# A load planner that charges for late loads by a graded curve, and the load order found with it

## The chip, the cores and the metric

The kernel runs on one core of a Trainium2 chip. The metric is the device time of one execution in microseconds (us). Before: 639.15 us, median of 4 runs (638.66 to 639.34). The experiments ran on three chips in as many sets of rounds, each with its own runs of before (medians 639.28, 638.76 and 639.18), so a kernel is compared by its ratio to before of the same rounds. A difference of two such ratios from different rounds is uncertain by about 0.25%, or 1.5 us.

## The reference

Two layers of attention with a KV cache and of a gated feed-forward block, each run twice with the same weights and the same caches, for four sequences and one new token.

```python
B, Sq, D = 4, 1, 512;  Hq, Hkv, Sk, Dh = 32, 8, 8192, 128;  F = 1792
x = A_x
x = x + attention(layernorm(x), k_cache, v_cache, wq, wo)   # layer 0
x = x + (silu(h @ w_gate) * (h @ w_up)) @ w_down             # h = layernorm(x)
x = x + attention(layernorm(x), k_cache, v_cache, wq, wo)   # layer 1, the same caches
x = x + feed_forward(layernorm(x))
```

Each cache is 64 MiB (4 x 8 x 8192 x 128 in bf16) and is read in both layers. SBUF holds only a small part of one.

## The kernel before

The caches are cut into units of 1 MB (1.049 MB in the profile's decimal count): half the rows of one head of one sequence, 8 KB in each of 128 partitions. SBUF has 11 slots for units (and 4 more in wq's place, once the last query is made). One DMA queue, issued from SyncE (SP), brings units into slots. A K unit is transposed in its slot by VectorE (2.3 us) and multiplied with the query by TensorE, a V unit is multiplied with the softmax by TensorE, and then the slot is free for a later load.

The code is shortened; `...` and the comments are this text's.

```python
def load_pair(u):                     # one unit; load_two does the same for two neighbours
    kind, l, b, g, cp = u             # K or V, layer, sequence, head, half
    def fn():
        s = PL.slot[home[u]]
        T.dma("sp", slot_sb(s), rows_of(u)[:, cp, :], sem_slot[s], writes=...)
    home[u] = u
    return PL.load(2.505, fn, u)
# ...
def t(hs): ...                        # k_pair: e.transpose(v, v) on DVE (L606)
def qk(): ...                         # 64 small matmuls into the score banks (L622)
st = PL.add("pe", 1.95, qk, tr + [qd, prev] + ..., prio, n=64)
if u not in kept_k:
    st.slot_of = home[u]              # after this step the slot is free
```

The order of loads is a string. `P` is two K units in one load, `K` one, `aBGH` a V unit of layer 0, `bBGH` one of layer 1, `A..` and `B..` two V units in one load, and `cBGH` a V unit of layer 1 that is *kept*: layer 0 left it in its slot, so nothing is loaded. `KM` says how many K units of each sequence are kept so. A kept unit saves 1 MB of reading and holds a slot meanwhile.

```python
ORDER = ("c100 c101 P c260 x P c300 c301 c261 wq P wg1 ... b360 b320 B35 B31 B33 b361 ")
KM = (4, 0, 0, 0)
```

Before the program is written, a planner runs through all steps with a duration for each, chooses slots and PSUM banks, and fixes the sequence of instructions on each engine. Each engine then works strictly in that sequence. The planner's times are used for these choices alone, and by whoever searched for the string. Its DMA model is this:

```python
LOAD_LEAD = 2.1
LOAD_TAIL = 2.1
# in pump(): t is when the load is issued, s.us how long its bytes take
dma_at = max(dma_at, t + self.LOAD_LEAD) + s.us    # end of transfer
s.end = dma_at + self.LOAD_TAIL                    # landing: what waits for it may start
```

## Time and profile before

| | before | how it is read |
|---|---|---|
| span of the profiled run | 636.9 us | first to last instruction of the core |
| cache and weight queue | 256.14 MB | the table of DMA queues |
| rate between the holes | 417 GB/s | table of stretches, 196 to 624 us |
| hole at the hand-over to layer 1 | 3.5 us | bytes missing against 417 GB/s, 184 to 196 us |
| last landing to end | 10.65 us | landing records: 626.25, span 636.9 |
| VectorE, TensorE busy | 63%, 62% | engine shares; neither is the bound |

One word is used throughout. The **lead** of a load is the time from its issue to the landing of the load before it in the queue. With a long lead, the bytes of this load follow those of its forerunner without a gap. Landings are read from the packed trace: a load has landed when its semaphore has had all of the load's 16 updates.

### The profile page before, as it was taken

To read this page: it belongs to the slowest core of one execution; us is meant where nothing else is said; L and a number is where in the kernel's file an instruction comes from. 1 tells how busy PE (TensorE), PEld (TensorE's weight loads), DVE (VectorE), ACT (ScalarE), POOL (GpSimd) and SP (SyncE) were. 2 spreads that over 40 slices of the span, in tenths; PEclk is the share of its full clock that TensorE was granted. 3 is DMA by queue.
4 is the path that set the end of the run, shared out by engine and by line. 5 is a ranking of instruction groups with operands and counts; after the bars stand their busy time and mean duration, and the time that the engine had idled before them with its cause. 6 is when DMAs were issued, how large, how long until landed. Compare 5 with 4: busy or idle time off the path is not lost.

```text
span 636.9 us, 18609 instructions
## 1 busy us (share of the span) xinstructions
PE 397.1 (62%) x8689; PEld 205.1 (32%) x8689; DVE 402.7 (63%) x615; ACT 40.4 (6%) x107; POOL 1.8 (0%) x8
## 2 busy tenths in 40 slices
PE   0375444454786675677576665578667676856686
PEld 0221211113542141135421241333431244721265
DVE  4477764365236958876579777366667863489832
ACT  1000200002000020000200100000100020000100
POOL 1000000000000000000000000000000000000000
PEclk9997686657557767667667778555575667568686
DMA  8999999999989999999999999999999999999991
GB/s 356 423 426 412 405 417 423 420 418 401 387 348 400 422 418 419 420 412 421 402 408 419 422 425 428 417 408 420 418 408 421 415 419 421 417 409 419 423 425 65
DMA packets 37237, 257.32 MB, mean 404 GB/s; under 512 B 3492, under 2 KB 9384, under 8 KB 10664
## 3 DMA queue, kind: packets, MB, share of 16 engines
q1 hardware_dynamic: 37160, 256.14, 97.7%
q8 instruction: 68, 1.11, 0.7%
q14 instruction: 9, 0.07, 0.0%
HBM read 256.12 MB, written 0.00 MB: 402 GB/s over the span
## 4 chain that ended last, share of the span: by engine, by line
DMA 63%; PE 18%; DVE 16%; issue 2%; SPq 0%; ACT 0%
DMA pool<-in_A_k_cache_dram 39%; DMA pool<-in_A_v_cache_dram 18%; DVE pool L606 12%; PE ps L622 7%; PE ps L763 5%; DMA wq_sb<-in_A_wq_dram 3%; PE ps L472 2%; DMA wo_sb<-in_A_wo_dram 2%; DMA wq_sb<-in_A_k_cache_dram 2%; DVE wq_sb L606 1%; PE ps L809 1%; PE ps L726 1%; DVE ps L790 1%; PE ps L681 1%; PE ps L873 1%
## 5 line engine op out<-in xcount | busy, mean ns | idle before, releaser
L606 DVE STREAM_TRANSPOSE pool<-pool 128x2048 uint32<-128x2048 uint32 x116 | 264.8, 2300 | 70.8 <-DMA pool<-in_A_k_cache_dram 70.6
L622 PE MATMUL ps<-pool,qpad 32*32 32x512 bf16 x3840 | 190.6, 543 | 127.2 <-DVE pool L606 120.7
L622 PEld LDWEIGHTS ps<-pool,qpad 32*32 32x32 bf16 x3840 | 54.6, 108 | 240.1 <-DVE pool L606 179.6
L763 PE MATMUL ps<-pool,pp 128*32 128x256 bf16 x1936 | 100.0, 366 | 43.1 <-DMA pool<-in_A_v_cache_dram 31.6
L763 PEld LDWEIGHTS ps<-pool,pp 128*32 128x32 bf16 x1936 | 57.5, 122 | 81.6 <-DMA pool<-in_A_v_cache_dram 42.8
L790 DVE STREAM_TRANSPOSE ps<-ps 128x256 f32<-128x256 f32 x62 | 28.4, 458 | 74.7 <-PE ps L763 74.4
L645 ACT ACTIVATE pp<-ps,negm 128x512 bf16<-128x512 f32 x32 | 21.6, 686 | 329.6 <-DVE negm L641 306.5
L726 PE MATMUL ps<-oT,wo_sb 128*128 128x4 bf16 x640 | 23.0, 167 | 12.6 <-DVE oT L794 9.2
L726 PEld LDWEIGHTS ps<-oT,wo_sb 128*128 128x128 bf16 x640 | 20.7, 103 | 24.7 <-DVE oT L794 16.7
L641 DVE TENSOR_REDUCE negm<-ps 128x1 f32<-128x512 f32 x32 | 19.9, 683 | 12.1 <-PE ps L622 12.1
L472 PE MATMUL ps<-xnT,wq_sb 128*128 128x4 bf16 x640 | 18.3, 166 | 12.1 <-DMA wq_sb<-in_A_wq_dram 11.4
L472 PEld LDWEIGHTS ps<-xnT,wq_sb 128*128 128x128 bf16 x640 | 17.7, 104 | 14.5 <-DMA wq_sb<-in_A_wq_dram 11.5
L606 DVE STREAM_TRANSPOSE wq_sb<-wq_sb 128x2048 uint32<-128x2048 uint32 x8 | 18.1, 2290 | 3.5 <-DMA wq_sb<-in_A_k_cache_dram 3.4
L681 PE MATMUL ps<-ident,pp 128*128 128x128 bf16 x128 | 16.0, 311 | 6.3 <-DVE pp L670 5.8
L622 PE MATMUL ps<-wq_sb,qpad 32*32 32x512 bf16 x256 | 13.2, 547 | 8.5 <-DVE wq_sb L606 8.5
L458 ACT ACTIVATE lnv<-var,eps_sb 128x4 f32<-128x4 f32 x10 | 3.0, 298 | 218.0 <-DVE var L453 218.0
L681 PEld LDWEIGHTS ps<-ident,pp 128*128 128x128 bf16 x128 | 12.7, 143 | 12.5 <-DVE pp L670 7.6
L792 DVE TENSOR_REDUCE osum<-ps 128x4 f32<-128x32 f32 x62 | 11.9, 191 | 2.1
L794 DVE TENSOR_TENSOR oT<-osum,invL 128x4 bf16<-128x4 f32 x62 | 10.5, 169 | 2.1
L670 DVE TENSOR_SCALAR pp<-pp,alpha 128x512 bf16<-128x512 bf16 x32 | 9.0, 346 | 1.8 <-ACT alpha L663 1.8
L690 ACT ACTIVATE pp<-ps 128x1024 bf16<-128x1024 bf16 x8 | 8.2, 1024 | 26.9 <-PE ps L681 26.9
L438 PE MATMUL ps<-xx,onesm 128*128 128x32 f32 x20 | 6.3, 410 | 5.3 <-DVE xx L433 4.3
(68 smaller groups left out, 149.4 us busy)
## 6 DMA issues: line engine op xcount, KB each, us to landing
pool<-in_A_k_cache_dram SPq DMA_DIRECT2D x86, 1024.0 KB, 9.7
pool<-in_A_v_cache_dram SPq DMA_DIRECT2D x82, 1024.0 KB, 10.0
pool<-in_A_k_cache_dram SPq DMA_DIRECT2D x15, 2048.0 KB, 15.8
pool<-in_A_v_cache_dram SPq DMA_DIRECT2D x10, 2048.0 KB, 16.6
wq_sb<-in_A_k_cache_dram SPq DMA_DIRECT2D x6, 1024.0 KB, 13.6
wq_sb<-in_A_wq_dram SPq DMA_DIRECT2D x1, 4096.0 KB, 22.0
wo_sb<-in_A_wo_dram SPq DMA_DIRECT2D x4, 1024.0 KB, 16.2
wq_sb<-in_A_k_cache_dram SPq DMA_DIRECT2D x1, 2048.0 KB, 10.3
```

The costliest lines, as they stand in the source:

```text
L472: op("pe", lambda e: e.matmul(ps[:, bk * BW + h * B:bk * BW + (h + 1) * B], lhsT=wq_sb[:, kt, h * Dh:(h + 1) * Dh], rhs=xnT[:, kt * B:(kt ...
L606: op("dve", lambda e: e.transpose(v, v), reads=keys, writes=keys)
L622: op("pe", lambda e: e.matmul(ps[32 * c:32 * (c + 1), a * BW:(a + 1) * BW], lhsT=qpad[rows, qbuf, es_, g, :], rhs=ap[h][rows, :, es_ // 2, ...
L641: op("dve", lambda e: e.tensor_reduce(negm[:, q, a:a + 1], bank(a), AX.X, ALU.max, negate=True), reads=[f"pb{a}"], writes=[f"negm{q}_{a}"])
L645: op("act", lambda e: e.activation(pblk(q)[:, :, a, :], bank(a).rearrange("p (t j) -> p t j", j=32), ACTF.Exp, bias=negm[:, q, a:a + 1], s ...
L670: op("dve", lambda e: e.tensor_scalar(seg, seg, alpha[:, q, a:a + 1], None, op0=ALU.mult), reads=[f"pp{q}_{a}", f"alpha{q}"], writes=[f"pp ...
L681: op("pe", lambda e: e.matmul(stg[:, t * P:(t + 1) * P], lhsT=pp[:, q, blk * P:(blk + 1) * P], rhs=ident[:], is_transpose=True, start=True ...
L726: op("pe", lambda e: e.matmul(ps[:, OPJ * BW + nq * B:OPJ * BW + (nq + 1) * B], lhsT=wo_sb[:, h, nq * P:(nq + 1) * P], rhs=oT[:, l, h, :], ...
L763: op("pe", lambda e: e.matmul(ps[32 * n:32 * (n + 1), bk * BW:bk * BW + 256], lhsT=pp[:, q, col:col + 32], rhs=v[:, 8 * f:8 * (f + 1), 32 ...
L790: op("dve", lambda e: e.transpose(blk, blk), reads=[f"pb{bk}"], writes=[f"pb{bk}"])
L792: op("dve", lambda e: e.tensor_reduce(osum[:], diag, AX.X, ALU.add), reads=[f"pb{bk}"], writes=["osum"])
L794: op("dve", lambda e: e.tensor_tensor(oT[:, l, g * REP:(g + 1) * REP, b], got, invL[:, q, g * REP:(g + 1) * REP], ALU.mult), reads=[f"pb{b ...
```

## The change

The intent, as far as the code shows it, is to charge a load by a graded curve of what a short lead costs, rather than by a hard limit, and to take an order and kept units found anew with it.

```diff
-    LOAD_LEAD = 2.1
+    LOAD_LEAD = 2.0
+    LOAD_SOFT = 1.05
+    LOAD_EASE = 3.7
     LOAD_TAIL = 2.1
...
+    def late(self, ahead):
+        if ahead < self.LOAD_LEAD:
+            return max(self.LOAD_LEAD - ahead, self.LOAD_SOFT)
+        return max(0.0, self.LOAD_SOFT * (self.LOAD_EASE - ahead) / (self.LOAD_EASE - self.LOAD_LEAD))
...
-                dma_at = max(dma_at, t + self.LOAD_LEAD) + s.us
+                dma_at += self.late(dma_at - t) + s.us
...
-ORDER = ("c100 c101 P c260 x P c300 c301 c261 wq P wg1 ...
+ORDER = ("P c200 x c201 c300 wq P c011 c260 P P a040 P c340 ...
-KM = (4, 0, 0, 0)
+KM = (2, 0, 0, 0)
...
-            return PL.load(4.914, fn, u0, u1)
+            return PL.load(4.924, fn, u0, u1)
-                return PL.load(2.505, fn, u)
+                return PL.load(2.51, fn, u)
```

## The prediction

> **What bounds the kernel now.** I read the page's engine shares and slice rows first. They say which resource is busy all the time.
>
> ```profile
> PE 397.1 (62%) x8689; PEld 205.1 (32%) x8689; DVE 402.7 (63%) x615; ACT 40.4 (6%) x107; POOL 1.8 (0%) x8
> ...
> DMA  8999999999989999999999999999999999999991
> GB/s 356 423 426 412 405 417 423 420 418 401 387 348 400 422 418 419 420 412 421 402 408 419 422 425 428 417 408 420 418 408 421 415 419 421 417 409 419 423 425 65
> ```
>
> No compute engine passes 63%. The DMA row is at 9 in all slices but the first, the twelfth and the last. So the kernel is one long read of the caches and weights, and its time is start + bytes over rate + holes in the stream + tail. The queue table gives the bytes, and the table of stretches (columns: length, then busy time of each engine with its instruction count, granted clock, DMA share, GB/s) gives rates and the one visible hole.
>
> ```profile
> q1 hardware_dynamic: 37160, 256.14, 97.7%
> ...
> 4.00:184.00 180.00, 91.12 (x2124) 48.17 (x2125) 99.77 (x145) 9.97 (x27) 0.00 (x0) 0.73 1.02 414
> 184.00:188.00 4.00, 3.02 (x60) 1.17 (x56) 2.54 (x2) 0.00 (x0) 0.00 (x0) 0.50 0.54 217
> 188.00:192.00 4.00, 4.00 (x116) 1.89 (x105) 0.82 (x3) 0.00 (x0) 0.00 (x0) 0.64 0.98 307
> 192.00:196.00 4.00, 2.48 (x104) 1.53 (x79) 0.00 (x0) 0.00 (x0) 0.00 (x0) 1.00 0.95 365
> 196.00:624.00 428.00, 286.97 (x6024) 143.43 (x6025) 295.32 (x441) 28.19 (x75) 0.00 (x0) 0.66 1.01 417
> 624.00:636.90 12.90, 9.47 (x314) 8.90 (x310) 3.99 (x22) 0.95 (x4) 0.00 (x0) 0.51 0.05 18
> ```
>
> Outside 184 to 196 us the stream runs at 414 to 417 GB/s, with the DMA share at 1. Inside it, (417 - 217) x 4 + (417 - 307) x 4 + (417 - 365) x 4 = 1448 KB are not moved, which is 1448 / 417 = **3.5 us**. The 12.9 us at the end are the last P·V products, the projection, the norm, the feed-forward part and the output. They need the last load and can't shrink by reordering.
>
> What opens the hole is in the chain that ended last (start, length, what) and in the timeline of the issuing queue:
>
> ```profile
> 165.11 0.18 DVE xx L889
> ...
> 174.56 2.07 PE ps L763 x25
> ...
> 180.93 1.88 PE ps L472 x64
> ...
> 184.05 0.98 PE ps L622 x16
> 185.03 0.98 issue
> 186.01 1.05 PE ps L622 x15
> ```
>
> ```profile
> 187.12 0.33 SPq L92 DMA_DIRECT2D pool<-in_A_v_cache_dram  x1
> ```
>
> The add of the attention result at 165.11 (L889) starts norm, feed-forward, norm and query projection (L472), with one V group of batch 1 in between (L763). The first score product of layer 1 (L622) ends at 187.06. It reads a kept K unit, and frees that unit's slot for the load issued at 187.12.
>
> **What the Trainium skill says.** "DMA: Bandwidth & Descriptors", section "Anatomy of one DMA — SWDGE (gpsimd) path", splits a DMA into a fixed part of about 2 us and a part that grows with the bytes. These loads are issued from SyncE, not GpSimd, but the hole looks like the same split: in the landing records the load before it was complete at 187.91 us, this load was issued at 187.12, only 0.79 us ahead, and it was complete at 193.66, 5.75 us after its forerunner instead of the usual 2.49. The loss of 3.25 us is larger than 2.0 - 0.79 = 1.2 us. The same page, "Rules for kernel authors", advises to issue a DMA early so that the setup overlaps. The trace agrees: the other cache loads were issued at least 3.9 us before their forerunner was complete, and none of them shows a loss of this kind. "TensorE: Matmul & The Clock Gate", section "What's actually happening", says that a little used TensorE runs at half clock. The table of stretches agrees (0.50 in 184 to 188), and the hand-over below is worked out at that clock.
>
> **The change, part by part.** It alters no instruction's form. It changes the planner's model of a late load, and with the new model another load order (a string of tokens), other kept units, and a little longer load constants were found. I take no time from either planner model, only counts and order of the emitted program.
>
> *Bytes.* A kept unit is a 1 MB half head of K or V that layer 0 leaves in SBUF for layer 1. Counting the tokens: before keeps 21 V and 4 K units, after keeps 22 V and 2 K units. So after loads one unit more: 232 instead of 231, and 257.19 MB instead of 256.14. At 417 GB/s this is 1.049 MB / 417 = **+2.5 us**, and it lies on the path, as DMA is the bound.
>
> *Pairs.* Double loads: 16 of K and 11 of V before, 16 and 11 after. No change. The loads for x and the weights are the same.
>
> *Compute.* Two kept K units fewer means two more DVE transposes at 2.3 us (4.6 us of DVE in 637, beside the stream, at 63%): **0**.
>
> *The hole at the first hand-over to layer 1.* Before, the slot for the late load is freed by the first kept K unit of layer 1, which waits for batch 0's whole projection, norm, feed-forward, norm and query chain. In the after program the same position looks alike: the last V pair of layer 0, batch 0 (loads number 44 and 45) gates the chain; behind it in the queue lie three weight pieces and seven V or K units (loads 46 to 55) whose slots are free in time; load 56 waits for the first kept K unit of layer 1. Work it out from the landing of load 45. P·V of one unit at half clock 1.05, the three DVE steps 0.9, the projection 0.6: 2.6 us. Then from the add (165.11 us in the chain of before) to the issue of the load that the kept unit frees (187.12) 22.0 us, 1.0 of which is an idle before L622 that may or may not come again. Together 23.6 to 24.6 us. The queue lasts from load 45's landing 7 x 2.5 for the units + about 7.4 for the pieces of wd, wu, wd (2.6, 2.3 and 2.5 in the landing records) = 24.9 us. So load 56 is issued 0.3 to 1.3 us ahead, much as the 0.79 of before: the hole stays, at an estimated 2 to 4 us: **-1.5 to +0.5 us**.
>
> *Other loads.* By the emitted order I counted, for each load, how much queue stands between the load that its slot's last user needs and itself. In before, 106 loads have four units (10 us) or less, in after 54. So after is no tighter in the steady stretches, but since these loads had 3.9 us or more to spare in before there is nothing there to win: **0**, with up to +1 if a hand-over of a later batch slips. What the remaining small dips cost (the instruction queue's 1.11 MB of fetches, the 1 KB rows of wo) is the same in both.
>
> *Start and tail.* wq is issued one double load (5 us) earlier, so the first scores start earlier; DMA is saturated then in any case: 0. The last loads (two pairs, then two halves) and the steps after them are the same: 0.
>
> Sum: 639.2 + 2.5 - 0.5 (middle of -1.5 to +0.5) = 641.2. The order was picked by a search that somebody then presumably timed, which argues for something that I don't see, so I lower it by 1.2 to **640.0 us**.
>
> **The rivals.** (1) The hole closes. If the hand-over in after has 2 us more to spare than I worked out (a faster clock in the chain, or a V unit of batch 1 done later), 3.5 us are won and 2.5 lost: 638.2. For it speaks that the new model charges late loads more smoothly, so the search should avoid them; against it, load 56's position. (2) The hole grows or a second one opens, say at the hand-over of batch 1 or 2, because the kept V units hold slots longer: 2.5 + 2 = 643 to 644. For it speaks that one slot is now held for V rather than K; against it, the slacker order in the middle. (3) Fewer bytes at a higher rate: more even issue lifts the steady rate from 417 towards the 428 of the best slice. 0.5% would be 3 us, giving 637 to 638. Against it: the DMA share is 1.00 or more in those stretches already, so there is no idle time to remove.
>
> **Range and chances.** The stream alone, 257.19 MB at 417 GB/s, takes 617 us; with 2 us of start and some 11 us after the last landing (626.25 to 636.9 us), 630 us is a floor at this rate, so 626.4 us (2% faster) is out of reach. 2% slower (652) would need four more holes. The rivals span 637 to 644, so I give **637.2 to 643.2** for 8 in 10, and 0.01 faster, 0.98 within 2%, 0.01 slower.
>
> **What would show it.** Queue 1 should show 257.19 MB, with 417 GB/s in the steady stretches. A hole of 2 to 4 us should stand near 175 to 190 us, ended by a load that waits for L622, and no other of over 1 us. The tail after the last load should be 10 to 11 us. I am wrong if the hole is gone and the time is under 637.2, which would mean that the chain's length in my sum (22.0 us) doesn't carry over; or if a later hand-over shows a dip below 350 GB/s.

## The result, and the profile after

After: 642.2 us, median of 4 runs (641.14 to 642.44), against 639.15 for before on the same chip. The ratio is 1.0046, with a 95% interval of 1.0028 to 1.0063. A ratio here is the mean time of one kernel's runs over that of the other's of the same rounds, so it is not quite the ratio of the medians. The change is slower by 1.8 to 4.0 us, clear of noise.

The slice rows and the queue table of after:

```profile
DMA  8999999999989999999999999999999999999991
GB/s 353 429 427 421 407 407 420 408 409 389 400 352 420 422 420 424 424 420 414 400 419 422 418 421 424 422 422 419 369 403 421 421 420 420 415 410 421 427 420 60
q1 hardware_dynamic: 37304, 257.19, 97.4%
```

The queue moved 257.19 MB, one unit of 1.05 MB more, and is as busy as before. There are two low places now: the slice of 352 and a new one of 369. The table of stretches of after (columns as in the prediction) shows them more finely:

```profile
172.00:176.00 4.00, 2.39 (x98) 2.08 (x103) 0.49 (x3) 0.00 (x0) 0.00 (x0) 0.50 0.85 350
176.00:180.00 4.00, 4.00 (x96) 1.76 (x80) 1.56 (x2) 0.00 (x0) 0.00 (x0) 0.64 0.49 139
180.00:184.00 4.00, 2.97 (x96) 1.60 (x80) 2.72 (x5) 0.00 (x0) 0.00 (x0) 1.00 0.98 410
...
188.00:456.00 268.00, 168.52 (x3674) 82.58 (x3674) 184.14 (x263) 14.71 (x40) 0.00 (x0) 0.68 1.01 419
456.00:460.00 4.00, 1.71 (x68) 1.44 (x68) 0.68 (x3) 0.00 (x0) 0.00 (x0) 0.50 0.94 365
460.00:464.00 4.00, 2.35 (x46) 1.60 (x36) 2.32 (x7) 1.60 (x5) 0.00 (x0) 0.72 0.78 279
464.00:468.00 4.00, 2.44 (x38) 1.12 (x39) 3.93 (x9) 1.37 (x5) 0.00 (x0) 0.70 1.02 365
468.00:624.00 156.00, 100.82 (x2319) 54.74 (x2316) 103.03 (x163) 10.49 (x26) 0.00 (x0) 0.71 1.01 419
```

The first hole lacks (69 + 280 + 9) x 4 = 1432 KB against 419 GB/s, or 3.4 us: as large as the 3.5 of before. The second lacks (54 + 140 + 54) x 4 = 992 KB, or 2.4 us. Before had 417 to 420 GB/s from 448 to 468 us. The 419 GB/s beside the second hole isn't a higher steady rate, because the hole has been cut out of it. With the hole in, after has the 417 of before over the same time; before has dips of its own there (350 GB/s from 308 to 312 us, 377 from 468 to 472), and is at 419, too, from 196 to 308 us.

```profile
200.00:624.00 424.00, 267.46 (x5992) 139.25 (x5976) 284.00 (x438) 28.16 (x75) 0.00 (x0) 0.70 1.01 417
```

The issuing queue's timeline in after has the late load of the first hole, and TensorE's timeline has what it waited for:

```profile
177.82 0.33 SPq L92 DMA_DIRECT2D pool<-in_A_k_cache_dram  x1
```

```profile
174.50 0.20 PE L492 MATMUL ps<-qT,ident 128*32 128x16 bf16 x2 [0.35 <-DVE qpad L552]
175.63 0.28 PE L492 MATMUL ps<-qT,ident 128*32 128x16 bf16 x14 [0.93 <-issue]
175.84 1.91 PE L629 MATMUL ps<-pool,qpad 32*32 32x512 bf16 x32
```

The load before it landed at 178.60 us, so its lead is 0.79 us. It lost 1.8 us (the late load of before lost 3.3 at the same lead); loads 58 and 60 lost the other 1.5 us of this hole. L629 is the score product (L622 of before, as the file is 7 lines longer): the first kept K unit of layer 1, at the end of norm, feed-forward and query, frees the slot, as before. Inside the query spread (L492) TensorE waited 0.93 us for nothing that the profile shows ("issue"). At the second hole the same thing happened, for longer:

```profile
456.63 0.67 PE L492 MATMUL ps<-qT,ident 128*32 128x16 bf16 x29
459.48 0.20 PE L492 MATMUL ps<-qT,ident 128*32 128x16 bf16 x3 [2.18 <-issue]
```

The V product behind it then freed a slot late: load 158 was issued at 460.73 us, 3.07 us ahead of a landing at 463.81. It lost 1.0 us. Load 161, with a lead of 4.61 us, lost another 1.0 us of this hole. Losses of 0.3 to 1.6 us at leads over 4 us stand in every full run's landing records, in before and after alike; their cause stays open.

From the last landings, the account is: before 626.25, after 629.64, which is +3.4 us in these two profiled runs. One unit more is +2.5, and +0.9 is left over. Counted in bytes moved by the same time, after is 1.2 us of reading ahead of before at 456 us and 1.0 us behind at 480, so the second hole is where the rest is lost. The time after the last landing is 10.65 and 10.76 us.

### The profile page after: what moved, and what is told of

Same layout as the page of the kernel before. It is cut to its first block, busy times and chain, and to the rows that moved or that the text cites. A ratio compares the mean times of both kernels' runs of the same rounds, so it can differ in the third digit from the quotient of the medians.

```text
span 640.4 us, 18612 instructions
## 1 busy us (share of the span) xinstructions
PE 387.2 (60%) x8689; PEld 200.7 (31%) x8689; DVE 405.9 (63%) x617; ACT 40.4 (6%) x107; POOL 1.8 (0%) x8
## 3 DMA queue, kind: packets, MB, share of 16 engines
q1 hardware_dynamic: 37304, 257.19, 97.4%
q8 instruction: 68, 1.11, 0.7%
## 4 chain that ended last, share of the span: by engine, by line
DMA 63%; DVE 17%; PE 17%; issue 2%; SPq 1%; ACT 0%
DMA pool<-in_A_k_cache_dram 32%; DMA pool<-in_A_v_cache_dram 26%; DVE pool L613 11%; PE ps L770 6%; PE ps L629 5%; DMA wo_sb<-in_A_wo_dram 3%; DMA wq_sb<-in_A_k_cache_dram 2%; DVE wq_sb L613 1%; PE ps L816 1%; PE ps L479 1%; DVE negm L648 1%; PE ps L733 1%; PE ps L688 1%; PE ps L880 1%; SPq L92 1%
## 5 line engine op out<-in xcount | busy, mean ns | idle before, releaser
L613 DVE STREAM_TRANSPOSE pool<-pool 128x2048 uint32<-128x2048 uint32 x118 | 269.1, 2298 | 78.8 <-DMA pool<-in_A_k_cache_dram 78.6
L629 PE MATMUL ps<-pool,qpad 32*32 32x512 bf16 x3840 | 187.6, 527 | 144.8 <-DVE pool L613 138.0
L629 PEld LDWEIGHTS ps<-pool,qpad 32*32 32x32 bf16 x3840 | 54.5, 106 | 257.1 <-DVE pool L613 196.4
L770 PE MATMUL ps<-pool,pp 128*32 128x256 bf16 x1936 | 94.9, 350 | 45.3 <-DMA pool<-in_A_v_cache_dram 37.9
L770 PEld LDWEIGHTS ps<-pool,pp 128*32 128x32 bf16 x1936 | 54.6, 117 | 78.9 <-DMA pool<-in_A_v_cache_dram 44.8
L733 PE MATMUL ps<-oT,wo_sb 128*128 128x4 bf16 x640 | 22.7, 166 | 11.3 <-DVE oT L801 7.3
L733 PEld LDWEIGHTS ps<-oT,wo_sb 128*128 128x128 bf16 x640 | 20.0, 102 | 24.6 <-DVE oT L801 15.0
L629 PE MATMUL ps<-wq_sb,qpad 32*32 32x512 bf16 x256 | 13.4, 553 | 10.0 <-DVE wq_sb L613 10.0
L688 PE MATMUL ps<-ident,pp 128*128 128x128 bf16 x128 | 14.6, 293 | 2.7 <-DVE wl L705 1.6
```

Source lines behind the costliest of these rows:

```text
L613: op("dve", lambda e: e.transpose(v, v), reads=keys, writes=keys)
L629: op("pe", lambda e: e.matmul(ps[32 * c:32 * (c + 1), a * BW:(a + 1) * BW], lhsT=qpad[rows, qbuf, es_, g, :], rhs=ap[h][rows, :, es_ // 2, ...
L688: op("pe", lambda e: e.matmul(stg[:, t * P:(t + 1) * P], lhsT=pp[:, q, blk * P:(blk + 1) * P], rhs=ident[:], is_transpose=True, start=True ...
L733: op("pe", lambda e: e.matmul(ps[:, OPJ * BW + nq * B:OPJ * BW + (nq + 1) * B], lhsT=wo_sb[:, h, nq * P:(nq + 1) * P], rhs=oT[:, l, h, :], ...
L770: op("pe", lambda e: e.matmul(ps[32 * n:32 * (n + 1), bk * BW:bk * BW + 256], lhsT=pp[:, q, col:col + 32], rhs=v[:, 8 * f:8 * (f + 1), 32 ...
```

## The experiments

Theories: the order (one unit more to read, and its hand-overs) costs the time; the planner's new curve favours it because it charges for leads that cost nothing. Rivals: the new model itself places instructions worse; compute sets the pace; the holes cost nothing in the end; the holes come from the length of the chain, not from page waits.

### One half of the change at a time

`old_model_new_order`: order, KM of after; planner of before.

```diff
 (before.py)
-ORDER = (before)      KM = (4, 0, 0, 0)
+ORDER = (after)       KM = (2, 0, 0, 0)
```

> The order and kept units of after, planned with the model of before. If the order (one unit more, and its hand-overs) makes the difference: 257.19 MB, slower than before by 2 to 4 us (641 to 643). Rival, that the new model itself places instructions and slots worse: near 639.

Measured: 641.76 us (641.26 to 642.65), ratio 1.0049 (1.0033 to 1.0065), 257.19 MB.

`new_model_old_order`: the converse, order and KM of before put into after.

> The order and kept units of before, planned with the model of after. If the order makes the difference: 256.14 MB, 639 within 1.5. Rival, that the model itself costs: 641 to 643. The new model would have it that this order is the worse one (3.9 us in its own count), so above 642.

Measured: 638.91 us (637.29 to 640.92), ratio 1.0006 (0.9987 to 1.0024), 256.14 MB. So the loss follows the order, and none that shows above the noise (0.24% at most) follows the model. The planner itself counted otherwise. (These counts come from running the planner of each kernel on the host.) With its new curve, it puts the end of the old order at 640.8 and of the new order at 636.9: an expected gain of 3.9. With the old model it had 632.2 and 634.3. The chip says +2.9 us (0.46% of 639). **The old model ranked the two orders rightly, and the new one the wrong way round.**

### What a short lead costs, by itself

`m_ahead`: a stream of 1 MB loads and nothing else. Every sixth load waits for a DVE transpose of a chosen length behind the third or fourth load before it, and so has a chosen lead. The output is wrong. It ran once, with a state that is unknown. The code is shortened to its sense.

```python
v = clock[:, 0:2 * cols].bitcast(uint32)
T.op("dve", lambda e: e.transpose(v, v), reads=[slot of load i - back], writes=["clock"])
T.dma("sp", pool[:, s, :], unit i, sem_slot[s], reads=["clock"], writes=[slot s])   # then 5 free loads
```

> Measures the disputed cost by itself: groups of six 1 MB loads with nothing else on the chip; the first load of each group waits until the load 3 or 4 before it is complete and a DVE transpose of chosen length is done, so it is issued about 7 to 0 us before its forerunner is complete (call that A). The new planner model (its 2.0 and 3.7 are counted without the landing tail of 2.1, so 4.1 and 5.8 in A) charges 0.0 at A = 5.8, 0.8 at 4.5, 1.05 at 3.5, 1.6 at 2.5, 3.3 at 0.8. The old one charges 0 down to 4.2 and then 4.2 - A: 0.7 at 3.5, 1.7 at 2.5, 3.4 at 0.8. My theory from the two traces (nothing lost at A of 3.57, 3.91, 4.6; 1.8 to 3.2 lost at 0.79): nothing lost above about 3.5, then about 3.5 - A: 1.0 at 2.5, 2.7 at 0.8. Wrong result on purpose.

Measured in the landing records. The loss is the time from the forerunner's landing to this one's, less the 2.485 us of loads in steady flow. The last column is after's curve as its planner applies it, at lead - 2.1.

| lead, us | loss in three trials, us | after's planner charges |
|---|---|---|
| 7.2, 6.2 | 0.0 in all six | 0 |
| 5.1, 4.7 | 0.0 in all six | 0.4, 0.7 |
| 4.2 | 0.0, 0.0, 0.7 | 1.0 |
| 3.7 | 0.0, 0.0, 0.0 | 1.05 |
| 3.1 | 0.0, 0.0, 0.9 | 1.05 |
| 2.6 | 1.8, 0.4, 0.0 | 1.5 |
| 2.0 to 2.1 | 3.0, 2.6, 1.2 | 2.0 |
| 1.5 to 1.6 | 1.1, 0.8, 1.4 | 2.6 |
| 1.0 | 1.8, 1.6, 1.7 | 3.1 |
| 0.44 | 2.2, 2.0, 2.1 | 3.7 |

My own "3.5 - lead" was too high below 2, and too simple around 2, where losses are largest and scatter. Before's hard limit, at the same leads, charges 4.2 - lead: nothing down to 4.2, then 0.5 at 3.7, 1.1 at 3.1, 1.6 at 2.6. The two models differ mainly between leads of 5.8 and 3.7, where after's charges up to 1.05 us and 11 of the 12 trials (at 5.1, 4.7, 4.2 and 3.7) lost nothing.

The curve in after starts to charge at 3.7 and reaches 1.05 at 2.0; read at the *landing*-based lead that is near the mean of the trials from 3.7 down to 2.6 (0.0, 0.4, 0.7 by the curve; 0.0, 0.3, 0.7 measured), and half of it around 2 (1.05 against 2.3). But the planner feeds it `dma_at - t`, and its landing comes only LOAD_TAIL = 2.1 us after `dma_at`. Thus it reads the curve 2.1 us too early. Where the curve came from isn't known, so that this is how it went wrong is an inference. That the charge is misplaced is measured, in this test and in the next paragraph.

In the trace of `new_model_old_order` (640.92 us, the slowest of its six runs) I set the planned against the measured for each load. Leaving out the start and the late load of the hand-over, the planner charged 50 loads 8.9 us in sum. On the chip the same 50 loads lost about 2 us in sum, 0.04 us each, and 1.5 of it at one load. The some 150 cache loads that it charged nothing lost 0.06 to 0.08 us each, more than those that it charged. The median measured lead is 2.25 us longer than the planned one. In the new order the planner charged only 15 such loads, 2.4 us in sum. So in the planner's account the new order wins because it avoids 6.5 us of charges, most of which do not exist, and it pays for that with one unit of real reading.

`lead_corrected`: the order of before in the new planner, with the curve moved to where the stream test put it.

```diff
-    LOAD_LEAD = 2.0
-    LOAD_EASE = 3.7
+    LOAD_LEAD = 0.2
+    LOAD_EASE = 1.5
+    LOAD_COLD = 0.5
-            return max(self.LOAD_LEAD - ahead, self.LOAD_SOFT)
+            return max(self.LOAD_COLD - ahead, self.LOAD_SOFT)
-ORDER = (after)      KM = (2, 0, 0, 0)
+ORDER = (before)     KM = (4, 0, 0, 0)
```

> Order and kept units of before, planned with a curve moved by the 2.1 us between the planner's end of transfer and the landing, as the stream test measured it (free above a planned lead of 1.5 us, 1.05 at 0.2, 0.5 minus the lead below). Theory: the curve in after is right in shape but read 2.1 us off, so it charged loads that cost nothing; with the shift it ranks the order of before ahead of the new one by 2.5 us, and the chip gives 639 within 1.5. Rival (the shift makes the plan too optimistic): above 641.

Measured: 638.68 us (638.03 to 638.93), ratio 0.9998 (0.9984 to 1.0011). As expected: the corrected curve does no harm, and its counts (629.4 for the old order, 631.9 for the new) differ by 2.5, close to the chip's 2.9. It gives no gain by itself either.

### Are the bytes on the path?

`two_short`: after, with two K loads of steady stretches cut to an eighth.

```diff
+SHORT = (("k", 1, 0, 7, 0), ("k", 1, 1, 7, 0))
+            if u in SHORT:
+                def fn(): T.dma("sp", slot_sb(s)[:, 0:512], rows_of(u)[:, cp, 0:512], sem_slot[s], writes=...)
```

> After with two loads of K in steady stretches (loads 67 and 120) cut from 8 KB to 1 KB a partition, the plan frozen; 1.84 MB less (255.35 MB). Wrong result on purpose. If each byte is on the path, a unit costs 2.49 us less the 0.37 that 128 KB in 1 KB rows takes (wo: 2.97 us for 1 MB), so 2 x 2.1 = 4.2 us are won: 638.0. Rival, that compute behind the loads sets the pace in these stretches: 641 to 642.

```profile
q1 hardware_dynamic: 37304, 255.35, 97.4%
```

Measured: 637.21 us (636.52 to 638.5), ratio 0.998 (0.9964 to 0.9996). Against the 1.0046 of after that is 0.66%, or 4.2 us, as expected from the bytes alone, with the 1.5 us of uncertainty said above. Bytes read in these stretches are on the path. (The result is meant to be wrong, but the comparison passed it: presumably the two cut units of 128 in layer 1 weigh too little to show.)

### The first hole

`short_chain`: after, the plan frozen, with 128 matmuls of the chain of sequence 0 left out.

```diff
+                nk = 1 if tag in ("q0_0", "q0_1") else KT               # query product, 96 of 128 left out
+                    nk = (1 if fo < 10 else 2 if fo == 10 else KT) if tag == "f0g0" else KT   # gate, 32 of 56
```

> After with the plan frozen, but 128 matmuls of batch 0's gate and query products left out (256 instructions, so the page boundaries of TensorE's instructions stay): the chain to layer 1 is about 3.7 us shorter. Wrong result on purpose. My theory: the load at the first hand-over is then issued 4 us or more ahead instead of 0.79, the hole at 176 to 188 us closes, and 3 us are won: 639.2. Rival, that the hole is time the stream would lose anyway (made up by later loads): 642.

The table of stretches of this run:

```profile
172.00:176.00 4.00, 3.87 (x88) 1.86 (x96) 0.30 (x2) 0.00 (x0) 0.00 (x0) 0.54 0.97 367
176.00:180.00 4.00, 0.97 (x32) 0.24 (x21) 1.60 (x1) 0.00 (x0) 0.00 (x0) 0.89 0.97 393
```

The stretch of 139 GB/s is gone. What is missing is (52 + 26) x 4 / 419 = 0.7 us instead of 3.4. Load 56 has a lead of 4.06 us, and lost nothing. (The lead grew by 3.3 us, and not quite as planned. The shorter gate product was partly lost again in a wait for a V unit, 1.34 us instead of 0.53. The shorter query product counted, and the wait of 0.93 us in the query spread was gone, too.) Measured: 639.65 us (638.88 to 640.46), ratio 1.0011 (0.9994 to 1.0029), 2.2 us (0.35%) less than after, uncertain by 1.6. So the hole does cost time at the end, and other loads don't make up for it.

`wo3_late`: after, with one token moved.

```diff
-wg1 wo3 a070 c351 a071 wd0 wu0 wd1
+wg1 a070 c351 a071 wo3 wd0 wu0 wd1
```

> After with one token moved: the last piece of wo is loaded behind the last V pair of batch 0 instead of ahead of it, so the chain to layer 1 starts from the landing of wo with 0.6 us of work before the add, not from V with 2.6. Right result, same bytes. Theory: lead of load 56 rises from 0.79 to about 2.8 us, the first hole falls by 1.5 to 3: 640. Rival (hole set by something other than the chain): 642.

Measured: 641.19 us (640.84 to 641.62), ratio 1.004 (1.0027 to 1.0053), and load 56 again had a lead of only 0.77 us. A miss. TensorE's timeline of this run tells why:

```profile
152.40 1.04 PE L770 MATMUL ps<-pool,pp 128*32 128x256 bf16 x16 [0.78 <-DVE pp L699]
153.74 0.59 PE L733 MATMUL ps<-oT,wo_sb 128*128 128x4 bf16 x16 [0.29 <-DMA wo_sb<-in_A_wo_dram]
154.25 1.04 PE L770 MATMUL ps<-pool,pp 128*32 128x256 bf16 x16
```

The last V pair was there by 150.7 us, but the plan puts a projection (L733), which needs the moved piece of wo, ahead of the second V product (L770). TensorE keeps to the sequence, so it stood until wo landed at 153.69, and the last V product came at 154.25 instead of 153.82. The wait changed its name, not its end.

### The second hole, and the pages

TensorE's instructions come in 68 fetches of 16 KB (256 instructions, 1.11 MB on queue 8). The DMA records of after show one start at 457.00 us, and TensorE's wait of 2.18 us is from 457.30 to 459.48. The packed traces settle that these waits belong to the fetches. Counting TensorE's recorded instructions in order, each of the 11 "issue" waits of 0.22 to 2.18 us that were looked up, in the hand-over chains of six runs, stands before an instruction whose number is 193 more than a multiple of 256, with shifted pages, too. They are called page waits from here on. Most of the 68 boundaries cost nothing that shows.

`page_shift`: after, with 128 more instructions at the very start, when TensorE has nothing to do. The same result.

```diff
-            for nq in range(NQ):                 # transposes of x
+            for nq in list(range(NQ)) * 17:
```

> After with the four transposes of x at the start repeated 17 times (64 matmuls, 128 instructions more on TensorE before anything else is ready; same result), which moves the boundaries of TensorE's 256-instruction pages by half a page, the plan frozen. Theory of the second hole (456 to 472 us): TensorE waited 2.18 us in the query spread of batch 2 for its next page, so the load behind it was issued only 3.07 us ahead. Then the waits move, this hole shrinks from 2.5 us to under 1.5, and the time falls by 0 to 1.5 us: 641.5. Rival, that the hand-over of batch 2 is late by its own length: same hole, 642.2.

The timeline of TensorE at the same place:

```profile
453.24 1.07 PE L479 MATMUL ps<-xnT,wq_sb 128*128 128x4 bf16 x35 [0.65 <-issue]
454.24 0.69 PE L492 MATMUL ps<-qT,ident 128*32 128x16 bf16 x32
454.87 1.90 PE L770 MATMUL ps<-pool,pp 128*32 128x256 bf16 x32
```

The query spread now runs through, and the wait, 0.65 us, sits in the query product. Load 158 had a lead of 6.09 us and lost nothing, and the second hole shrank to dips above 360 GB/s: from 456 to 480 us the mean is 395 GB/s instead of 375, so 1.4 us are missing against 419 instead of 2.5. At the first hole the wait of 0.93 us went away too, load 56 had a lead of 1.97 us, and 1.9 us are missing (352 and 291 GB/s from 172 to 180 us) instead of 3.4. Measured: 639.95 us (639.84 to 640.54), ratio 1.0022 (1.0008 to 1.0037), 0.24% or 1.5 us less than after. This difference of two ratios is as large as its uncertainty. `wo3_late`, whose moved token changed the lead by nothing, ran in the same rounds: 641.19 us, 1.2 us more, and the two ranges don't touch. Hence the page phase, which no one chose, is worth about 1.2 to 1.5 us here, up to half of what the change lost.

That suggested the same for before:

> Before (its own planner, order and plan) with the transposes of x repeated 9 times: 64 instructions more on TensorE at the start, same result, so its 256-instruction page boundaries move by a quarter page. In before, TensorE waited for pages twice in the chain to layer 1 (0.85 us at 172.51, 0.98 at 185.03). Theory: what falls on the chain depends on the phase alone. If both go, load 57 is issued 2.6 us ahead instead of 0.79, the hole of 3.5 us shrinks to about 1, and the time falls to 636 to 637.5; if they come back at other places of the chain, 639. Rival (page waits don't matter): 639 in both phases.

> The same with 17 times, 128 instructions, half a page. In after half a page won 2.2 us. Theory: 636 to 637.5 if the page waits leave the chain, 639 if they come back in it; rival: 639.

`before_page_64` (before, with `* 9`): 638.24 us (637.92 to 638.31), ratio 0.9985 (0.9971 to 0.9998). The page waits came back in the chain, 0.46 and 1.54 us, and load 57 had a lead of 0.95 us, so the hole stayed (3.2 us by its stretches). That it was 1.0 us faster than before all the same isn't explained; the interval nearly reaches 1.

`before_page_128` (before, with `* 17`): 637.05 us (636.61 to 637.6), ratio **0.9968** (0.9956 to 0.9981). The chain has one wait of 0.22 us left, load 57 a lead of 3.31 us, and the stretches are:

```profile
184.00:188.00 4.00, 3.94 (x88) 1.80 (x96) 2.43 (x3) 0.00 (x0) 0.00 (x0) 0.50 0.82 279
188.00:192.00 4.00, 4.00 (x138) 2.17 (x144) 0.89 (x4) 0.00 (x0) 0.00 (x0) 0.80 0.95 383
```

Together they lack (138 + 34) x 4 / 417 = 1.6 us instead of 3.5. Against `before_page_64` of the same rounds, which also has more matmuls at the start but kept its page waits, it is 1.2 us faster, and the ranges don't touch. This version, before plus 64 idle-time matmuls, beats both kernels: 2.0 us less than before, and 0.78% or 5 us less than after. It is a matter of luck with the phase, though: any instruction added ahead of the chain moves it again.

(A search of some 40,000 orders from each kernel with the corrected curve is said to have given no better order to try. This is not shown.)

## Why the prediction was right, and where it was not

The measured 642.2 us lies in the range of 637.2 to 643.2, near its upper end. By its steps:

- **Bytes, +2.5:** right. 257.19 MB was read, the unit cost agrees with `two_short`, and the loss follows the order.
- **Pairs, compute, start, tail, 0:** right. The tail differs by 0.1 us, and two transposes more did not show.
- **The first hole stays, lead of 0.3 to 1.3:** right. The lead is 0.79 us, the idle of about 1 us in the chain came again (0.93), and the hole is 3.4 us by rate. So this term was nearly 0, within the -1.5 to +0.5. The chain time of 22.0 us was carried over from before with two page waits in it (0.85 and 0.98 us), of which the prediction saw one; after took 21.3 us from the add (156.50) to the issue (177.82), with one. The half clock was there again (0.50 from 172 to 176 us). That low use is its reason isn't shown: in the prediction's own table TensorE was busy for 3.02 of 4 us at a clock of 0.50, and for 2.48 of 4 us at 1.00.
- **Other loads, 0 with up to +1 if a later hand-over slips:** the +1 came, as +0.9 at the last landing. "No other of over 1 us" in the last paragraph was wrong: the second hole lacks 2.4 us by rate. So one of the prediction's own signs of being wrong came: a later hand-over below 350 GB/s (279 from 460 to 464 us). The cause that rival 2 named, kept V units holding slots longer, is not what the trace shows. It was a page wait of 2.18 us for the part at load 158, as `page_shift` confirmed; the part at load 161 stays open. That the +1 fits is luck as to its cause.
- **Minus 1.2, since somebody presumably timed the new order:** this step failed. Without it the sum was 641.2, nearer to the truth. The order was presumably found with the new model, which charges for leads that cost nothing, so that it was chosen said little about the chip.
- **Rival 3, a higher steady rate:** not seen. From 200 to 624 us both kernels have 417 GB/s.

What I had not expected at all is that the new model ranks the two orders the wrong way round; the prediction only said that there was nothing to win in leads of 3.9 us or more, which `m_ahead` bore out but for one of its trials (0.7 us lost at a lead of 4.2).

## What to carry to other kernels

In a kernel whose one DMA queue is nearly always full, count the bytes first. Here one unit of 1 MB more was 2.5 us, and only a real hole can pay for it. A planner's penalty has to be measured on the same clock as the planner counts (end of transfer or landing), and checked load by load against a trace, before a search is let loose on it. And where an engine works in a fixed sequence, look for its unexplained "issue" waits in the one serial chain that opens the hole: the page phase of its instructions may be worth nearly as much as a new order (here 2.0 us against 2.9).

## What the Trainium skill lacked or had wrong

- "Runtime: NRT & Kernel Launch", section "Instruction fetch mechanics", says that crossing a 16 KiB boundary is "mostly hidden". The 68 fetches of 256 instructions are seen as it says, but in dense stretches of small matmuls TensorE waited 0.85, 0.93, 0.98 and 2.18 us in the traces of before and after, always at the same place of a 256-instruction page, and shifting the phase by 128 instructions changed the time by 1.2 to 1.5 us in one kernel and 2.0 in the other.
- "DMA: Bandwidth & Descriptors" gives a fixed cost of about 2.0 us for the GpSimd path and no such total for loads from SyncE, and no page that I read says how early a load from SyncE must be issued behind a full queue. Here a 1 MB load was free in every trial at a lead of 4.7 us or more, in 7 of 9 trials from 4.2 down to 3.1 (0.7 and 0.9 us lost in the other two), lost most around 2 us (1.2 to 3.0), and 2.1 us at a lead of 0.44. That last is 5.0 us from issue to landing (0.44 + 2.49 + 2.1), so an estimate of the fixed part is about 2.6 us.
- Its table of measured rates, for DMAs issued from GpSimd, has 6.15 us for 1 MB, and none that I read has the time of one such load from SyncE. Here the first 1 MB load of `m_ahead`, with only the 4 KB of x ahead of it in the queue, landed 5.1 us after its issue, and in the full queue the same size followed every 2.49 us.
